# Between the forward and the backward recurrence: row turns in other PSUM banks, loads ahead of crossbar transposes, the last 64 rows moved back, buffers laid out anew

## The chip, the cores and the metric

One NeuronCore of one Trainium2 chip runs the whole program. The metric is the device time in microseconds (us) of one execution. Before the change three executions took 4788.9, 4787.57 and 4790.88 us, with a median of 4788.9 us.

## The reference, cut to what matters

The program computes a block with a memory-augmented attention and a gated feed-forward part, and the gradients of all its inputs. The attention is a recurrence over 64 segments of 32 tokens: each segment sees 8 memory rows and its own 32 rows, and the first 8 rows of its output are the memory of the next segment.

```python
for s in range(n_seg):                                   # 64 segments
    h = concatenate([mem, x[:, s*32:(s+1)*32]], axis=1)   # 8 + 32 rows, D = 640
    q, k, v = h @ Wq, h @ Wk, h @ Wv                      # 32 heads of 128
    p = softmax(where(mask, q @ k.T * scale, -1e9))
    o = (p @ v) @ Wo                                      # 4096 -> 640
    mem, out = o[:, :8], o[:, 8:]
out = x + s * silu(swiglu(xn))                            # s: the attention's output
_, vjp = jax.vjp(f, x, mem0, Wq, Wk, Wv, Wo, w1, w3, w2); grads = vjp(grad_out)
```

## The kernel before, in words

The program is a sequence of phases that share little at their borders. The two that matter here are the forward recurrence, function `recurrence`, and the backward recurrence, function `phase4_Abwd`. Each consists of a serial chain over the 64 segments (`chain`), in whose gaps independent work is placed by hand: `in_order` ties every instruction to its written place on its engine, so each engine runs its list in order and a waiting instruction holds up all that is written behind it on that engine. The DMA queues too are such lists: SP's (`nc.sync`), ScalarE's (`nc.scalar`) and GpSimd's, POOL in the profile (`nc.gpsimd`).

The work in the gaps is attention for the token rows. Three segments make a tile `tl` of 120 rows (96 token rows and 24 memory rows), and a tile has 8 units `(tl, qd)` of 4 heads. A unit goes through: load of q rows (`ld("q", ...)`, tile xq, two buffers), transposes on TensorE (`turn_q`, qpt, L757), scores (xsp), softmax (`soft`, `norm`), transposes of the probabilities (`turn_p`, xpp), product with v (`pv`, xpo), and a store of the output rows into the DRAM array OR. All these PSUM tiles share one ring of five banks, tag "x". The other three banks, bA, bB and bC, belong to the chain.

The stretch between the loops is what the change is about. When the forward chain ends, 13 units (`tail`) still have no scores. They are run in a loop of 15 iterations, and `fill()` calls between their steps draw pieces of other work out of a generator `work1`:

- `out_proj`: the output projection of token rows in blocks of 128 rows. An item is one block and one group of 4 heads, and a block has 8 items. Its OR rows are loaded by POOL into one of four slices `orow` of tile vt, three items ahead (L508). `turn` transposes them (L518) into bC, VectorE copies them into a half of oTm (L519), and 8 matmuls against Wo accumulate the item into bA and bB (L525). After 8 items s_tok is copied out and stored into SR.
- `wq_turn`: 32 head blocks of Wq are transposed on TensorE (L719), also into bC, and copied to WqT.
- `gx_block`: blocks of upstream gradient rows (g0x in this phase, gx in the next; loaded as a crossbar transpose from GS) times WoT into bA and bB (L1045), copied to g0st or gstg and stored in GX0 (called GX in the profile).
- `w_ld`: one piece of a weight that is loaded transposed by the crossbar (`turned_load`, DMA_TRANSPOSE, L270, always on SP's queue). WoT has 16 pieces and WkT has 16.

Rows 1344 to 1855 go through `out_proj` inside the loop, two gradient blocks (rows 1920 to 2047 and 1824 to 1919) follow in the last iterations, and `op(X1, S)`, rows 1856 to 2047, is the last work of the phase.

`phase4_Abwd` begins with small tables (`bdm`, built in gox), zeroed buffers (L1091, and krb at L1398) and a prologue of 19 units of backward attention: per unit `ld` (tiles gqv, gor and gPr, in a ring of six, of which two lie in krb), `turn` (L1290, L1297), `dprob`, `dsoft`, `gmem`, with the other four gradient blocks in between (`gx_work`), and 8 loads of WvT on SP. Before the chain starts, the first ride of token rows (gride) is loaded and copied to gox by POOL (L1113).

SBUF space is handed out by pools. A tile of the new phase that lies over a tile of the old one waits until the old one's users are done.

Of the kernel before, what the change touches and what calls it, by code (L numbers as in the profile page):

```python
# [9 lines left out]
BF16 = mybir.dt.bfloat16  # L10
# [6 lines left out]
P = 128  # L17
# [474 lines left out]
        in_order(k, start)  # L492


def out_proj(k, Wo, x0, x1, acc, pb, orow, oTs, stok, q):

    nc = k.nc
    items = [(x, min(P, x1 - x), qd) for x in range(x0, x1, P) for qd in range(8)]

    def ld(i):  # L500
        if i >= len(items):
            return
        x, w, qd = items[i]
        a = 0
        while a < w:
            tl, r = divmod(x + a, 96)
            n = min(96 - r, w - a)
            q.dma_start(orow[i % len(orow)][a:a + n, :], k.OR[120 * tl + r:120 * tl + r + n, 512 * qd:512 * qd + 512])  # L508
            a += n

    def turn(i):
        if i >= len(items):
            return
        x, w, qd = items[i]
        r = orow[i % len(orow)]
        pt = bview(pb, P, 4, w, bf=True)
        for j in range(4):
            nc.tensor.transpose(pt[:, j, :], r[0:w, j * P:(j + 1) * P], k.ident[0:w, 0:w])  # L518
        nc.vector.tensor_copy(oTs[i % 2][:, :, 0:w], pt)  # L519
# [24 lines left out]


def recurrence(k, W0, W4, Wv, Wk_, Wq, Wo, kTs, vt, hxs, qTs, xPs, PTs, oTm):
    nc, tc = k.nc, k.tc
    D, DC, S, H, HD, T = k.D, k.DC, k.S, k.H, k.HD, k.T
    with tc.tile_pool(name="achain", bufs=1) as ch, \
# [421 lines left out]
        op = lambda x0, x1: out_proj(k, Wo, x0, x1, (bA, bB), bC, orow, oTs, stok, nc.gpsimd)  # L971
        X0, X1 = k.GB0, k.GB0 + 4 * P
        assert X1 <= 96 * (k.NTL - 3) + 96 + 96

        def work1():
            w_alloc("q")
            o = op(X0, X1)
            next(o)
            yield
            for h in range(H):  # L980
                next(o)
                wq_turn(h)
                yield
                next(o)
                yield
            next(o, None)
            w_alloc("k")
            for i, (x0, w) in enumerate(k.GXB[0:2]):
                xs = ch.tile([P, DC, P], BF16, name="g0x", tag=("oride", "fup")[i])
                gx_ld(k, xs, x0, w)  # L990
                for cg in range(4):
                    sg = ch.tile([P, 1024], BF16, name="g0st", tag="stg", bufs=2)
                    for b in range(2):
                        gx_block(k, xs, sg, (bA, bB)[b], WT["o"], x0, w, cg, b, nc.gpsimd)
# [7 lines left out]
        ld("q", *tail[0])  # L1002
        ld("q", *tail[1])
# [13 lines left out]
        ld("q", *tail[3])  # L1017
        ld("v", *tail[0], nc.gpsimd)
        for i in range(len(tail) + 2):
            w_ld(1 if i < 4 else 0)  # L1020
            for f, o, n in ((turn_q, 2, 1), (lambda *u: ld("q", *u), 4, 0), (scores, 1, 1), (soft, 0, 0),
                            (lambda *u: norm(*u, nc.vector), 0, 0), (turn_p, -1, 1), (lambda *u: pv(*u, nc.scalar), -2, 2),
                            (lambda *u: ld("v", *u, nc.gpsimd), 1, 0)):
                if 0 <= i + o < len(tail):
                    f(*tail[i + o])
                fill(n)
        for _ in work:
# [23 lines left out]
def phase4_Abwd(k, out2, W4, WT):  # L1051
# [20 lines left out]
    with tc.tile_pool(name="gst", bufs=1) as st, tc.tile_pool(name="gchain", bufs=1) as ch, \  # L1072
# [2 lines left out]
            tc.tile_pool(name="gpm", bufs=1, space=bass.MemoryType.PSUM) as psm:  # L1075
        NG = 4

        bdm = st.tile([P, 16, 8], BF16, name="bdm")
        goxs = [st.tile([P, DC, 32], BF16, name=f"gox{i}") for i in range(2)]
        bdf = goxs[0][:, 0:4, :].rearrange("p a b -> p (a b)").rearrange("p (a b) -> p a b", b=8)  # L1080
        b16 = st.tile([P, 16], F32, name="b16")
        nc.gpsimd.memset(bdf, 0.0)
        nc.gpsimd.affine_select(out=bdf, in_=bdf, compare_op=ALU.not_equal, fill=1.0, base=0,
                                pattern=[[-1, 16], [-16, 8]], channel_multiplier=1)
        nc.vector.tensor_reduce(b16[:], bdf, axis=AX.X, op=ALU.add)
        nc.vector.tensor_copy(bdm[:], bc_last(b16[:], 8))
        gOTs = [st.tile([P, 4, P], BF16, name=f"gOT{i}") for i in range(2)]
        gors = [st.tile([120, 512], BF16, name=f"gor{i}") for i in range(NG)]
        gdSs = [st.tile([120, 4, P], BF16, name=f"gdS{i}") for i in range(2)]
        for tt in goxs + gOTs + gors + gdSs:  # L1090
            nc.vector.memset(tt[:], 0.0)  # L1091
        krb = st.tile([120, 2, 2048], BF16, name="krb")
        bA, bB, bC = [psm.tile([P, 512], F32, name=f"gbank{i}") for i in range(3)]
        pm = bA
        nc.sync.dma_start(k.m_rows(k.GWO, T - 1).rearrange("r (c d) -> (r c) d", d=160),
                          goxs[(T - 1) % 2][0:32].rearrange("p a b -> p (a b)"))
        rides = {}
        WARM = dict(G4=1)

# [15 lines left out]
        def loads(t):  # L1115
            tl, s = t // 3, t % 3
            ns, nm, nx, n = k.geo(tl)
            vT = ch.tile([P, H, 40], BF16, name="vTt", tag="vTt", bufs=1)
# [19 lines left out]
            krs[t] = kr  # L1138

        def load_xp(t):  # L1140
            xp = ch.tile([P, 8, 2, 32], F32, name="xp", tag="xp", bufs=1)
# [116 lines left out]
        def ld(tl, qd, eng=None):  # L1258
# [6 lines left out]
            g = i % 6 if early else (i - len(pro) + 1) % NG  # L1265
            if g < NG:
                gor = gors[g][:]
                qv = fl.tile([120, 2, 512], BF16, name="gqv", tag="gqv", bufs=4)[:]
                Pr = fl.tile([120, 4, P], BF16, name="gPr", tag="gPr", bufs=4)[:]
# [125 lines left out]
            return gap  # L1395
        todo = pro + todo

        nc.vector.memset(krb[:], 0.0)  # L1398
        xb = krb
        gx = ch.tile([P, 2, DC, P], BF16, name="gx0", tag="vTt", bufs=1)  # L1400

        def gx_work():
            blocks = k.GXB[2:]
# [3 lines left out]
            n = 0  # L1407
            for i, (x0, w) in enumerate(blocks):
                for cg in range(4):
                    sg = ch.tile([P, 1024], BF16, name="gstg", tag=("gstg", "xp")[cg % 2], bufs=1)  # L1410
# [815 lines left out]
```

## Time and profile before

| | us |
|---|---|
| median of three runs (lowest, highest) | 4788.9 (4787.57, 4790.88) |
| the profiled execution | 4788.32 |
| its span in the profile | 4786.6 |
| TensorE (PE) busy in the span | 4491.6 (94%) |
| last PE work before the stretch's first idle time ends at | 1603.36 |
| last matmul of the forward phase ends at | 1790.7 |
| first matmul of the backward chain starts at | 1886.5 |

Times inside the program are us from the span's start. PE is the matmul stream and PEld its weight loads, DVE is VectorE, ACT is ScalarE, SPq and ACTq are the queues in which these engines issue DMAs. "Idle before" or "waited for" says how long an engine stood still and what ended the wait. A line number is that of the kernel before. The granted clock (PEclk) is the share of full speed that TensorE was given.

### The profile page before, as it was taken

The numbers are of one execution on the slowest core, as the hardware profiler recorded it, in microseconds if no ns is written. First come the engines' busy times: TensorE is split into PE (matmuls) and PEld (weight loads), VectorE is DVE, ScalarE is ACT, GpSimd is POOL, SyncE is SP. The second block draws the span as 40 slices with busy tenths as digits, with TensorE's granted clock in tenths as the row PEclk, the third lists the DMA queues.
The fourth block names the chain that finished last, engine by engine and source line by source line (L and its number), as shares of the span: only waits on it lengthen the run. The fifth ranks groups of instructions, "written<-read, shape, count | busy, mean of one in ns | idle before, by whom it ended". The sixth has DMA issues, their size and how long they took to land. (4 is left out here: it accounts for less than half of the span.)

```text
span 4786.6 us, 160294 instructions
## 1 busy us (share of the span) xinstructions
PE 4491.6 (94%) x64504; PEld 2828.7 (59%) x64504; DVE 2246.8 (47%) x7157; ACT 1588.3 (33%) x4360; POOL 2148.4 (45%) x3622
## 2 busy tenths in 40 slices
PE   8998999999999677999999998899999999999999
PEld 4544555555555444666666665666667666666675
DVE  8734666666666424555555553332234322311460
ACT  5432555555544323333333332332233322300000
POOL 6532555555555443445444443653345533411340
PEclk9998999999999898999999999999999999999999
DMA  8773665665555647777777774844355443669673
GB/s 266 231 241 109 180 179 175 178 183 177 176 169 168 149 109 216 202 215 212 213 209 207 210 208 117 213 133 119 107 149 159 132 118 108 184 205 213 153 182 98
DMA packets 972138, 834.82 MB, mean 174 GB/s; under 512 B 518547, under 2 KB 853399, under 8 KB 969433
## 3 DMA queue, kind: packets, MB, share of 16 engines
q1 hardware_dynamic: 757551, 543.98, 40.7%
q0 software_dynamic: 133392, 234.80, 16.6%
q10 hardware_dynamic: 80451, 45.78, 3.7%
q8 instruction: 509, 8.34, 0.8%
q14 instruction: 235, 1.92, 0.1%
HBM read 472.66 MB, written 310.33 MB: 164 GB/s over the span
## 5 line engine op out<-in xcount | busy, mean ns | idle before, releaser
L1600 PE MATMUL wg<-gr,hr 128*128 128x512 bf16 x2400 | 521.7, 379 | 0.0
L1581 PE MATMUL g<-w,ghacc 128*128 128x320 bf16 x3072 | 458.4, 300 | 0.8
L1600 PEld LDWEIGHTS <-hr 128*128 128x128 bf16 x2400 | 234.1, 98 | 278.7
L1581 PEld LDWEIGHTS <-ghacc 128*128 128x128 bf16 x3072 | 288.0, 98 | 103.8 <-ACT ghacc L92 2.2
L306 PEld LDWEIGHTS <-hx 128*32 128x32 bf16 x7680 | 177.1, 96 | 172.8 <-issue 10.1
L90 DVE CAST wgo<-wg 128x512 bf16<-128x512 f32 x72 | 49.8, 692 | 471.2 <-PE wg L1600 471.2
L872 POOL DMA_DIRECT2D OR<-xv x163 | 89.9, 551 | 369.7 <-ACT xv L92 344.6
L90 DVE CAST stg<-bank 128x512 bf16<-128x512 f32 x256 | 177.0, 692 | 165.3 <-PE bank L306 154.0
L1546 POOL DMA_DIRECT2D GSP<-grs x48 | 25.7, 550 | 471.4 <-ACT grs L1538 470.5
L92 ACT COPY ghacc<-t6g 128x768 bf16<-128x768 bf16 (+1 forms) x176 | 137.1, 779 | 296.9 <-PE t6g L1563 294.4
L1294 POOL DMA_DIRECT2D VTD<-gvT x176 | 129.7, 743 | 227.9 <-ACT gvT L1293 204.1
L325 PEld LDWEIGHTS <-gkv 128*8 128x8 bf16 x8192 | 179.5, 87 | 82.8 <-DVE gkv L1165 2.6
L804 ACT ACTIVATE xP<-xsp,xnm 120x120 bf16<-120x120 f32 (+1 forms) x540 | 186.1, 373 | 31.2 <-DVE xnm L786 28.6
L824 POOL TENSOR_TENSOR xP<-xP,xrz 120x480 bf16<-120x480 bf16 x163 | 161.3, 990 | 75.8 <-DVE xrz L823 46.9
L1587 DVE TENSOR_TENSOR ghacc<-ghacc,g 128x320 f32<-128x320 f32 x192 | 93.5, 487 | 209.4 <-PE g L1581 209.4
L92 ACT CAST wgo<-wg 128x512 bf16<-128x512 f32 x48 | 28.1, 585 | 479.8 <-PE wg L1600 421.4
L1323 DVE SCALAR_TENSOR_TENSOR gdS<-gdp,Dx,gPr 120x120 bf16<-120x120 f32 (+1 forms) x680 | 182.9, 331 | 0.0
L1341 POOL DMA_DIRECT2D GXP<-gks x157 | 91.2, 581 | 195.7 <-ACT gks L1339 187.0
L325 PE MATMUL gbank<-WvT,gkv 128*8 128x320 bf16 x4096 | 173.0, 314 | 0.1
L325 PE MATMUL bank<-Wo,oTm 128*32 128x320 bf16 x4032 | 154.8, 308 | 18.5 <-DVE oTm L676 18.5
L306 PE MATMUL bank<-Wq,hx 128*32 128x512 bf16 x2560 | 163.3, 384 | 5.4 <-DVE stg L90 5.4
L325 PE MATMUL gbank<-WkT,gkv 128*8 128x320 bf16 x4096 | 162.2, 299 | 2.4 <-DVE gkv L1165 1.8
(363 smaller groups left out, 10983.9 us busy)
## 6 DMA issues: line engine op xcount, KB each, us to landing
QVS<-stg SPq DMA_DIRECT2D x128, 256.0 KB
gqv<-QVS SPq DMA_DIRECT2D x108, 192.0 KB
vTt<-VTD SPq DMA_DIRECT2D x64, 320.0 KB
PR<-xP POOLq DMA_DIRECT2D x168, 120.0 KB, 3.1
VTD<-gvT POOLq DMA_DIRECT2D x168, 120.0 KB, 3.8
DSR<-gdS POOLq DMA_DIRECT2D x168, 120.0 KB, 3.2
dS<-DSR SPq DMA_DIRECT2D x168, 120.0 KB
P<-PR SPq DMA_DIRECT2D x168, 120.0 KB
```

The source lines that it names most:

```text
L90: return nc.vector.tensor_copy(out, in_)
L92: return nc.scalar.copy(out, in_)
L306: k.nc.tensor.matmul(bank[32 * g:32 * g + 32, :], x[:, dc, :], W[:, dc, c0:c0 + 512], start=(dc == 0), stop=(dc == k.DC - 1), tile_positio ...
L325: k.nc.tensor.matmul(pm[p0:p0 + nq, 0:320], x[:, h, :], W[:, h, 320 * b:320 * b + 320], start=(first and i == 0), stop=(last and i == 15), ...
L804: nc.scalar.activation(Pb[0:n, j, 0:n], sp[0:n, j, :], ACT.Exp, bias=nmx[0:n, j:j + 1], scale=k.scale, accum_out=Z[0:n, j:j + 1])
L824: eng.tensor_tensor(Pb[0:n, :, 0:n], Pb[0:n, :, 0:n], bc_last(rz[0:n], n), ALU.mult)
L1294: nc.gpsimd.dma_start(k.VTD[tl][:, :, h0:h0 + 4, :], vTq[:])
L1323: nc.vector.scalar_tensor_tensor(dS[0:n, j, 0:n], dp[0:n, j, :], Dx[0:n, j:j + 1], Pr[0:n, j, 0:n], op0=ALU.subtract, op1=ALU.mult)
L1341: (nc.sync if (tl, qd) in pro else nc.gpsimd).dma_start(k.GXP[tl, :, qd, 0:ns], ks[:].rearrange("p s i h m -> p s i (h m)"))
L1581: nc.tensor.matmul(pg[:], ring[:, i, j, r0:r0 + P], Ws[qd][i][:, j, 320 * h:320 * h + 320], start=(i == 0 and j == 0), stop=(i == 2 and j ...
L1587: nc.vector.tensor_tensor(a, a, pg[:], ALU.add)
L1600: nc.tensor.matmul(pw[:], hr[:, tl, dc * P:(dc + 1) * P], grs[i][:, tl, :], start=(tl == 0), stop=(tl == NF - 1))
```

## The change: what it does

1. `out_proj` transposes its rows into a tile of the five-bank ring (`obank`) and no longer into bC. bC is left to `wq_turn`.
2. In the last segment's gaps, 4 pieces of WoT are issued where there were 12 by the end of the chain. The q rows of the first two tail units are issued there (gap G1), ahead of the pieces. The other 12 pieces go one per iteration behind the loads of that iteration, and 16 of WkT follow when `wq_turn` is through (Wq's place becomes WkT's).
3. `out_proj` runs 5 blocks, rows 1344 to 1983, inside the loop. Both gradient blocks run behind the loop, and the last 64 rows (1984 to 2047) behind them, with their first three loads issued ahead of the gradient blocks. The first gradient block is loaded (`g_ld(0)`) ahead of WkT's pieces, the second behind them.
4. In `phase4_Abwd` the buffers are static and laid out in another order; krb (120 x 4096 bf16) is zeroed by POOL at the head of its queue and not by VectorE; bdm, the zeroing of gox and its DMA are put off to iteration 8 (`chain_consts`); the loads of four units stand ahead of the gradient rows (gx) on SP.

```diff
-def out_proj(k, Wo, x0, x1, acc, pb, orow, oTs, stok, q):
+def out_proj(k, Wo, x0, x1, acc, bank, orow, oTs, stok, q, done):
...
-        pt = bview(pb, P, 4, w, bf=True)
+        pt = bank(w)
...
                 if t == T - 1:
                     if g == "G1":
                         w_alloc("o")
-                    if g in ("G1", "G2", "G4", "G5"):
-                        w_ld(3)
+                        ld("q", *tail[0])
+                        ld("q", *tail[1])
+                    if g in ("G2", "G4"):
+                        w_ld(2)
...
+        obank = lambda w: ps.tile([P, 4, w], BF16, name="opt", tag="x", bufs=5)
-        X0, X1 = k.GB0, k.GB0 + 4 * P
+        X0, X1 = k.GB0, k.GB0 + 5 * P
...
-            for h in range(H):
-                next(o)
-                wq_turn(h)
-                yield
-                next(o)
-                yield
-            next(o, None)
-            w_alloc("k")
+            for _ in o:
+                if n % 2 == 0 and n < 2 * H:
+                    wq_turn(n // 2)
+                n += 1
+                yield
+                if n == 2 * H:
+                    g_ld(0)
+                    while wfetch:
+                        w_ld(1)
+                    w_alloc("k")
+                elif n > 2 * H:
+                    w_ld(1)
+            g_ld(1)
+            o = op(X1, S)
+            next(o)
             for i, (x0, w) in enumerate(k.GXB[0:2]):
-                xs = ch.tile([P, DC, P], BF16, name="g0x", tag=("oride", "fup")[i])
-                gx_ld(k, xs, x0, w)
...
+            for _ in o:
+                yield
...
         for i in range(len(tail) + 2):
-            w_ld(1 if i < 4 else 0)
...
+            if not WT.get("k"):
+                w_ld(1)
...
-        for _ in op(X1, S):
-            w_ld(1)
-        while wfetch:
-            w_ld(1)
...
+        gors = [st.tile([120, 512], BF16, name=f"gor{i}") for i in range(NG)]
+        gqvs = [st.tile([120, 2, 512], BF16, name=f"gqv{i}") for i in range(NG)]
+        gOTs = [st.tile([P, 4, P], BF16, name=f"gOT{i}") for i in range(2)]
+        vTb = st.tile([P, H, 40], BF16, name="vTt")
...
+        krb = st.tile([120, 2, 2048], BF16, name="krb")
...
-        for tt in goxs + gOTs + gors + gdSs:
+        for tt in gOTs + gors + gdSs:
             nc.vector.memset(tt[:], 0.0)
...
-        nc.vector.memset(krb[:], 0.0)
+        nc.gpsimd.memset(krb[:], 0.0)
...
         work = gx_work()
+        for _ in range(4):
+            ld_next()
         next(work)
-        for _ in range(6):
+        for _ in range(2):
             ld_next()
...
             if i == 8:
+                chain_consts()
                 ride_ld(T - 1)
                 ride(T - 1)
```

More of the change, by code (lines that the diff above doesn't have):

```diff
@@ L507, in ld @@
             n = min(96 - r, w - a)
+            assert tl < k.NTL - 2 or (tl, qd) in done
             q.dma_start(orow[i % len(orow)][a:a + n, :], k.OR[120 * tl + r:120 * tl + r + n, 512 * qd:512 * qd + 512])
@@ L970, in recurrence @@
         stok = lambda: ch.tile([P, D], BF16, name="s_tok", tag="oride")
-        op = lambda x0, x1: out_proj(k, Wo, x0, x1, (bA, bB), bC, orow, oTs, stok, nc.gpsimd)
-        X0, X1 = k.GB0, k.GB0 + 4 * P
-        assert X1 <= 96 * (k.NTL - 3) + 96 + 96
+        obank = lambda w: ps.tile([P, 4, w], BF16, name="opt", tag="x", bufs=5)
+        done = {(k.NTL - 2, qd) for qd in SPL[0]}
+        op = lambda x0, x1: out_proj(k, Wo, x0, x1, (bA, bB), obank, orow, oTs, stok, nc.gpsimd, done)
+        X0, X1 = k.GB0, k.GB0 + 5 * P
         def work1():
@@ L979, in work1, with g_ld @@
             yield
-            for h in range(H):
-                next(o)
-                wq_turn(h)
-                yield
-                next(o)
-                yield
-            next(o, None)
-            w_alloc("k")
+            g0 = []
+            def g_ld(i):
+                xs = ch.tile([P, DC, P], BF16, name="g0x", tag=("fup", "oride")[i])
+                gx_ld(k, xs, *k.GXB[i])
+                g0.append(xs)
+            n = 0
+            for _ in o:
+                if n % 2 == 0 and n < 2 * H:
+                    wq_turn(n // 2)
+                n += 1
+                yield
+                if n == 2 * H:
[8 more added lines that the diff above has]
+            next(o)
             for i, (x0, w) in enumerate(k.GXB[0:2]):
-                xs = ch.tile([P, DC, P], BF16, name="g0x", tag=("oride", "fup")[i])
-                gx_ld(k, xs, x0, w)
                 for cg in range(4):
@@ L993, in work1 @@
                     for b in range(2):
-                        gx_block(k, xs, sg, (bA, bB)[b], WT["o"], x0, w, cg, b, nc.gpsimd)
+                        gx_block(k, g0[i], sg, (bA, bB)[b], WT["o"], x0, w, cg, b, nc.gpsimd)
                         w_ld(1)
                         yield
+            for _ in o:
+                yield
         def fill(n=1):
@@ L1001, in recurrence @@
         work = work1()
-        ld("q", *tail[0])
-        ld("q", *tail[1])
         fill()
@@ L1025, in recurrence @@
                     f(*tail[i + o])
+                    if o == -2:
+                        done.add(tail[i + o])
                 fill(n)
+            if not WT.get("k"):
+                w_ld(1)
+        assert next(work, 0) is None
         for _ in work:
             pass
-        for _ in op(X1, S):
-            w_ld(1)
-        while wfetch:
-            w_ld(1)
+        assert not wfetch
         in_order(k, start)
@@ L1076, in phase4_Abwd @@
         NG = 4
+        gors = [st.tile([120, 512], BF16, name=f"gor{i}") for i in range(NG)]
+        gqvs = [st.tile([120, 2, 512], BF16, name=f"gqv{i}") for i in range(NG)]
+        gOTs = [st.tile([P, 4, P], BF16, name=f"gOT{i}") for i in range(2)]
+        vTb = st.tile([P, H, 40], BF16, name="vTt")
+        goxs = [st.tile([P, DC, 32], BF16, name=f"gox{i}") for i in range(2)]
         bdm = st.tile([P, 16, 8], BF16, name="bdm")
-        goxs = [st.tile([P, DC, 32], BF16, name=f"gox{i}") for i in range(2)]
+        xpb = st.tile([P, 8, 2, 32], F32, name="xp")
+        gPrs = [st.tile([120, 4, P], BF16, name=f"gPr{i}") for i in range(NG)]
+        gdSs = [st.tile([120, 4, P], BF16, name=f"gdS{i}") for i in range(2)]
+        krb = st.tile([120, 2, 2048], BF16, name="krb")
         bdf = goxs[0][:, 0:4, :].rearrange("p a b -> p (a b)").rearrange("p (a b) -> p a b", b=8)
         b16 = st.tile([P, 16], F32, name="b16")
[L1082 to L1089, printed above, removed]
-        for tt in goxs + gOTs + gors + gdSs:
+        for tt in gOTs + gors + gdSs:
             nc.vector.memset(tt[:], 0.0)
-        krb = st.tile([120, 2, 2048], BF16, name="krb")
         bA, bB, bC = [psm.tile([P, 512], F32, name=f"gbank{i}") for i in range(3)]
         pm = bA
-        nc.sync.dma_start(k.m_rows(k.GWO, T - 1).rearrange("r (c d) -> (r c) d", d=160),
-                          goxs[(T - 1) % 2][0:32].rearrange("p a b -> p (a b)"))
         rides = {}
@@ L1117, in loads @@
             ns, nm, nx, n = k.geo(tl)
-            vT = ch.tile([P, H, 40], BF16, name="vTt", tag="vTt", bufs=1)
+            vT = vTb
             nc.sync.dma_start(vT[:], k.VTD[tl][:, s])
@@ L1140, in load_xp @@
         def load_xp(t):
-            xp = ch.tile([P, 8, 2, 32], F32, name="xp", tag="xp", bufs=1)
+            xp = xpb
             nc.sync.dma_start(xp[:], k.GXP[t // 3, :, :, t % 3])
@@ L1267, in ld @@
                 gor = gors[g][:]
-                qv = fl.tile([120, 2, 512], BF16, name="gqv", tag="gqv", bufs=4)[:]
-                Pr = fl.tile([120, 4, P], BF16, name="gPr", tag="gPr", bufs=4)[:]
+                qv, Pr = gqvs[g][:], gPrs[g][:]
             else:
@@ L1396, in phase4_Abwd, with chain_consts @@
         todo = pro + todo
-        nc.vector.memset(krb[:], 0.0)
+        def chain_consts():
+            nc.gpsimd.memset(bdf, 0.0)
+            nc.gpsimd.affine_select(out=bdf, in_=bdf, compare_op=ALU.not_equal, fill=1.0, base=0,
+                                    pattern=[[-1, 16], [-16, 8]], channel_multiplier=1)
+            nc.vector.tensor_reduce(b16[:], bdf, axis=AX.X, op=ALU.add)
+            nc.vector.tensor_copy(bdm[:], bc_last(b16[:], 8))
+            for tt in goxs:
+                nc.gpsimd.memset(tt[:], 0.0)
+            t = T - 1
+            nc.sync.dma_start(k.m_rows(k.GWO, t).rearrange("r (c d) -> (r c) d", d=160),
+                              goxs[t % 2][0:32].rearrange("p a b -> p (a b)"))
+        nc.gpsimd.memset(krb[:], 0.0)
         xb = krb
-        gx = ch.tile([P, 2, DC, P], BF16, name="gx0", tag="vTt", bufs=1)
+        gx = vTb[:].rearrange("p h c -> p (h c)").rearrange("p (i a b) -> p i a b", i=2, a=DC)
+        xs2 = xpb[:].rearrange("p a b c -> p (a b c)").bitcast(BF16)
         def gx_work():
@@ L1409, in gx_work @@
                 for cg in range(4):
-                    sg = ch.tile([P, 1024], BF16, name="gstg", tag=("gstg", "xp")[cg % 2], bufs=1)
+                    sg = ch.tile([P, 1024], BF16, name="gstg", tag="gstg", bufs=1)[:] if cg % 2 == 0 else xs2
                     for b in range(2):
```

## The prediction, made before the changed kernel ran

> **What bounds the kernel now.** I read the 40 slices of the page first, then busy time by stage, then waits and queues inside the stretch that the diff touches.
>
> ```profile
> PE   8998999999999677999999998899999999999999
> ```
>
> TensorE is busy nearly everywhere, so a gain must come from its few idle places. Slices 14 to 16 (6, 7, 7) are the stretch between the loops. Cut at the ends of its stages (us; PE, PEld, DVE, ACT and POOL busy, PE clock, DMA share, GB/s):
>
> ```profile
> 1603.40:1623.70 20.30, 0.00 (x0) 0.02 (x1) 0.72 (x2) 0.58 (x1) 7.28 (x13) 0.50 1.12 217
> 1624.00:1723.70 99.70, 77.34 (x808) 53.90 (x806) 34.82 (x104) 43.01 (x149) 49.91 (x97) 0.95 0.38 94
> 1723.70:1790.70 67.00, 46.48 (x292) 26.71 (x292) 13.25 (x34) 8.24 (x21) 23.09 (x45) 0.90 0.62 142
> 1790.70:1886.50 95.80, 65.05 (x620) 38.56 (x619) 45.60 (x258) 31.94 (x110) 35.17 (x60) 0.80 0.76 226
> ```
>
> PE stands idle for 20.3, 22.4, 20.5 and 30.8 us: first at the start, then in the tail loop, then in the crossbar and last-row stage, then in the backward prologue. No other engine is near full, so these are waits. The list of waits for 1595 to 1890 (waiter, what it waited for: total us, times, longest):
>
> ```profile
> PE qpt L757 <- DMA xq<-QVS: 20.3, 1, 20.3
> PE bank L518 <- DMA vt<-OR: 12.9, 5, 6.9
> PE bank L719 <- DVE oTm L519: 11.8, 10, 2.0
> PE bank L1045 <- DMA g0x<-GS: 10.0, 2, 7.1
> PE gvpt L1290 <- DMA gqv<-QVS: 8.2, 1, 8.2
> POOL gox L1113 <- DMA gride<-GS: 11.9, 1, 11.9
> ```
>
> SP's and POOL's queues at the start (start us, duration, engine, line):
>
> ```profile
> 1601.29 5.87 SPq L270 DMA_TRANSPOSE WoT<-in_A_Wo_dram  x3
> 1607.25 0.53 SPq L604 DMA_DIRECT2D QVS<-stg  x1
> 1607.83 12.75 SPq L270 DMA_TRANSPOSE WoT<-in_A_Wo_dram  x6
> 1620.63 0.72 SPq L245 DMA_DIRECT2D xq<-QVS  x1
> ...
> 1611.49 0.56 POOL L571 DMA_DIRECT2D QVM<-QVS  x1 [4.71 <-DMA QVS<-stg]
> 1612.04 3.06 POOL L508 DMA_DIRECT2D vt<-OR  x6
> ```
>
> A crossbar piece holds SP for about 2 us, and the first q load stands behind nine. POOL's OR loads wait separately, behind QVM, which waits for a store that SP held back too.
>
> **The change part by part.**
>
> *Start.* SP's order becomes: two q units (4 DMAs, about 2.2 us), v loads (2.3), two pieces (3.8), the QVS store, two pieces. From 1593.1 the q loads are out by 1595.3 and the store goes at about 1602, instead of 1607.25. It landed 4.2 us after issue (1607.25 to 1611.49), so by about 1606.2. POOL's queue is then at QVM anyway (its QM issue is at 1606.20), and the OR loads start near 1607.3 instead of 1612.04. The first item's two take 1.0 us to issue and 2.5 (median landing in the loop) to 5.3 (here, beside the pieces) to land: 1611 to 1613.6. Transposes of q no longer wait, but the first row turn does, until about 1612 instead of 1624.06: **-12 us** (-9 to -15). The idle time shrinks to about 8 us; it is not gone.
>
> *Tail loop.* In bC each turn waited for the other kind's copy; the 11.8 us in ten waits go. Their cover is good: in the new order a row turn's copy is needed only an item later. In exchange the ring of five takes 6.5 tiles per iteration and not 4. One tile, the score bank, is held from `scores` to the last exp. The program's waits show a row turn behind `pv` waiting for just that exp in some iterations. The exps of a unit are 4 x (0.38 + 0.2) us and its max is 0.65, about 3 us after its place, when PE has done about 3 us of other work. The trace has no such wait, so I bound it: 0, or 1 us in each of 15 iterations; I take 3 us, since ACT is busy for 43 of 99.7 us. The waits for OR in the loop (1.9 and 2.5 us) and the 3.3 us for s_tok remain. One crossbar piece per iteration of about 7.6 us, behind that iteration's loads, is covered by two iterations of lead on q. Net **-9 us** (-14 to 0). The eight items moved into the loop cost what they cost before, 8 x (1.25 + 0.06 us seen between items): no gain or loss.
>
> *Crossbar and last rows.* Idle waits here are 7.1 + 2.9 us for g0x, 6.9 + 1.0 for OR, 1.5 for a g0st buffer. They come from PE running out of other work while SP needs 13.65 + 15.80 us for WkT's 16 pieces. After the change the pieces start when the last Wq block is turned (at 1720.9 before), and 9 items (9 x 1.6), the rest of attention (4), and the first gradient block (10) lie beside them: 28.4 us against 29.5. The second gradient block's load stands behind all pieces and needs 2.9 us (1727.92 issue to 1730.80 use): about 4 us of wait. The last 64 rows' loads are covered by the gradient blocks; in their queue the fourth stands behind the last GX store, about 1.5 us. Here a rule and a row part. The Trainium skill (DMA: Bandwidth & Descriptors, Anatomy of one DMA — SWDGE path, two cost components) puts one DMA at 2.0 us plus bytes over 436 GB/s, an estimate of 2.2 us for a load of 96 KB: three items ahead (4.9 us) hides each OR load beside the pieces at no cost. The trace's list of DMA issues has medians of 2.5 us in the loop (1640 to 1720) but 5.3 us beside WoT's pieces (1595 to 1625); with 1 us of issue that exceeds 4.9 by 1.4 us, for up to 9 items: 12 us. By the rule 0, by the row at most 12; I take 4, because the wait also lets SP's pieces get ahead and so comes off the 4 us of g0x. GX stores meet the pieces as before: 3 us. So 4 + 1.5 + 4 + 3 = 12.5 less 1 of overlap = 11.5 us instead of 20.5: **-9 us** (-18 to +3). Waits of 7 us went with slow clock (0.72 in the 10 us after the first, 0.66 around the second); of the low-clock time in the middle two stages (about 5% of 77 and 10% of 46 us, 8.5 us), I take half back: **-4 us** (-7 to 0).
>
> *Border.* Before, the last matmul ends at 1790.7 and the first turn starts at 1798.96. New: both copies of s_tok (0.48 us), SR's issue, its landing 2.0 us later (2.6 in all). The new program has SP, VectorE and POOL all wait for that. On POOL krb's memset comes next, ahead of the four QVM loads. Here is the second rule: the skill (VectorE: DVE Perf Modes, Zero memsets can be issued as uint32) says a memset takes a cycle per element and that VectorE may clear two bf16 as one word. It speaks against this edit, and the trace has both forms:
>
> ```profile
> L1398 DVE MEMSET krb<- 120x2048 uint32 x1 | 1.8, 1765 | 0.4 <-issue 0.4
> L475 POOL MEMSET kT<- 128x3840 bf16 x1 | 3.3, 3317 | 0.0
> ```
>
> By the POOL row 4096 elements take 3.54 us. If POOL cleared words too it would be 1.8, and the border would stay at 8.2. By the row: 2.6 + 3.54 + 3.3 (landing of gqv<-QVM) = 9.4: +1.2 us. The gradient rows now stand behind twelve loads, which took 6.55 us (1796.40 to 1802.95): 2.7 + 6.55 + 2.9 = 12.2 us after the end, where the first gradient matmul began after 8.96. PE is full from there to 1827, so this shifts the prologue: **+3.2 us**, the 1.2 inside it (0 to +5).
>
> *Prologue.* The 8 WvT loads and their DMA share of 0.9 stay. `chain_consts` adds to POOL and VectorE some 1.5 us (the tables took 0.20, 0.40, 0.23 and 0.24; two memsets 0.24 each) in front of gox, but POOL stood 11.9 us there, waiting for gride. That cover holds. On SP one small DMA (0.3 us), with its wait for the memset, is put ahead of gride, so that chain ends later: **+1 us** (0 to +3). The removed table work stood beside SR's landing and gives nothing.
>
> Sum: -12 - 9 - 9 - 4 + 3.2 + 1 = -29.8 us. The profiled execution took 4788.32 us, 1.7 around its span, so 4758.5; the median is 0.6 above it, so 4759.
>
> **The rivals.**
>
> *The loop's gain is eaten beside the pieces.* WkT's 29.5 us are fixed. If PE arrives early it waits for the second g0x, and OR loads at 5.3 us stall it: the third stage gives nothing, nor do 3 us of clock. -30 + 9 + 3 = -18: 4771 us. For it: DMA share 1.0 to 1.1 in 1730 to 1760. Against: 14 us of moved projection now lie there.
>
> *Only the start's q loads help.* If the QVS store, between the pieces, lands as late as before, OR loads start at 1612, the row turn at 1618: -6; with the loop's 9 lost to the ring, border and prologue at +8: -6 - 9 - 1 + 8 = -8, 4781 us, no change. This is also the case that the change does not do what it says: waits only move to the next release.
>
> *Slower: the ring of five.* Every one of 48 row turns takes a ring bank. If each waits for the exp that frees a score bank, in-order PE, VectorE and ScalarE run in step. Gain without it is 33 us (3 were charged already), so it decides from 33/48 = 0.7 us per turn. At 1.1 us: 53 - 33 = +20, 4809 us. For it: 6.5 tiles in five banks. Against: in the loop before, no wait of PE for a ring tile or for bC was over 2.0 us, and ScalarE is 43% busy.
>
> **How the numbers follow.** Forecast (-45 to -21) 0.57; eaten beside the pieces (-21 to -10) 0.24; no change (within 9.6 us, 0.2%, about what a measurement of this kernel can tell from none) 0.09; the ring, slower, 0.10. Faster 0.81, same 0.09, slower 0.10. The range takes the first two cases to their ends: 4744 to 4779.
>
> **What would show it.** Right: the wait of xq (20.3) gone and PE's first idle time about 8 us, released by vt<-OR; no oTm wait at L719's successor; last forward matmul some 34 us earlier; the border wait on gqv near 9.4 us and the first gx matmul about 12 us after the end; krb's memset 3.5 us on POOL. Wrong: idle time of row turns in the ring (opt) above 10 us in sum, a g0x wait above 10 us, or a prologue over 105 us.

## The result, and the profile after

| | before | after |
|---|---|---|
| median of 9 runs, us | 4792.89 (4779.51 to 4804.0) | 4769.33 (4759.59 to 4779.03) |
| profiled execution, us | 4788.32 | 4766.39 |
| span of that execution, us | 4786.6 | 4764.5 |

The runs of before here are those of the front table and six more. The ratio is 0.9951 (95% interval 0.9936 to 0.9966): faster, by about 24 us. The forecast was 4759, its range 4744 to 4779.

The changed kernel by stage (each cut is at the same piece of work as before: PE's last work before the idle time, its first work after it, the end of the last Wq block's turn, the last forward matmul, the first matmul of the backward chain; given are length; PE, PEld, DVE, ACT and POOL busy; PE clock, DMA share, GB/s). The stages are the idle start, the tail loop, the crossbar and last rows, and the border with the prologue:

```profile
1606.80:1614.08 7.28, 0.01 (x1) 0.03 (x1) 0.36 (x2) 0.69 (x2) 6.28 (x12) 0.50 0.94 231
1614.08:1711.65 97.57, 74.83 (x807) 54.21 (x808) 34.55 (x103) 42.35 (x147) 53.91 (x105) 0.94 0.58 129
1711.65:1770.30 58.65, 46.80 (x292) 26.49 (x290) 13.27 (x33) 8.43 (x21) 19.96 (x39) 0.88 0.74 153
1770.30:1868.50 98.20, 64.20 (x609) 38.42 (x616) 44.11 (x255) 31.42 (x110) 39.12 (x63) 0.80 0.74 221
```

With before cut at the same events (1603.37, 1623.71, 1723.12, 1790.71, 1886.49), the stages went from 20.34 to 7.28 us, from 99.41 to 97.57, from 67.59 to 58.65, and from 95.78 to 98.20. These four differences, -13.1, -1.8, -8.9 and +2.4, make -21.4 of the span's -22.1. The odd one is the second: PE's idle time in the loop is 97.57 - 74.83 = 22.7 us, where it was 99.41 - 77.09 = 22.3. The list of PE's waits, 1595 to 1870 (waiter, what it waited for: total us, times, longest), says what took the place of oTm:

```profile
PE opt L519 <- DMA vt<-OR: 28.7, 17, 7.3
PE gvpt L1303 <- DMA gqv<-QVM: 9.2, 1, 9.2
...
PE gbank L1062 <- DMA vTt<-GS: 4.1, 1, 4.1
PE bank L1062 <- DVE g0st L90: 4.1, 1, 4.1
...
PE bank L1062 <- DMA g0x<-GS: 2.3, 1, 2.3
```

The waits of 20.3 us for xq and of 11.8 us for oTm are gone. The row turns' waits for rows in the loop alone, after and then before:

```profile
PE opt L519 <- DMA vt<-OR: 24.3, 14, 7.3
PE bank L518 <- DMA vt<-OR: 5.0, 3, 2.5
```

Of the 24.3 us, 7.3 are the start's, which leaves 17.0 us where before had 5.0. So the time that PE had spent waiting for oTm was not saved; PE now waits for the next thing that is late. GpSimd's timeline in the loop shows how the rows come (start, duration, line, in brackets the idle time ahead and what ended it):

```profile
1653.38 1.03 POOL L509 DMA_DIRECT2D vt<-OR  x2
1658.34 0.55 POOL L826 DMA_DIRECT2D PR<-xP  x1 [3.92 <-ACT xv L92]
1658.88 1.01 POOL L509 DMA_DIRECT2D vt<-OR  x2
...
1703.46 0.54 POOL L826 DMA_DIRECT2D PR<-xP  x1 [5.69 <-ACT xP L805]
1703.99 1.01 POOL L509 DMA_DIRECT2D vt<-OR  x2
```

No row load is issued for over 4 us at the first place, and for over 6 us at the second, because the store of P ahead of it in GpSimd's order waits. PE turns an item's rows about every 3 us (33 such turns in the 97.6 us). A lead of three items, some 9 us, is then in large part used up before the load is issued. The longest wait for rows inside the loop follows the second place. It ends with the pair of loads issued at 1703.99, for the next pair leaves only at 1706.00:

```profile
1706.86 0.39 PE L519 MATMUL opt<-ident,vt 128*128 128x128 bf16 x4 [4.09 <-DMA vt<-OR]
```

PE was ready for these rows at 1702.77, before their loads were issued.

### The profile page after: what moved, and what is told of

Read it like the earlier page. It is cut to its first block, busy times and chain, and to the rows that moved or that the text cites. A ratio compares the mean times of both kernels' runs of the same rounds, so it can differ in the third digit from the quotient of the medians.

```text
span 4764.5 us, 159990 instructions
## 1 busy us (share of the span) xinstructions
PE 4452.5 (93%) x64223; PEld 2829.8 (59%) x64504; DVE 2245.4 (47%) x7154; ACT 1587.8 (33%) x4360; POOL 2152.3 (45%) x3625
## 3 DMA queue, kind: packets, MB, share of 16 engines
q0 software_dynamic: 133392, 234.80, 16.6%
## 5 line engine op out<-in xcount | busy, mean ns | idle before, releaser
L325 PEld LDWEIGHTS <-gkv 128*8 128x8 bf16 x8192 | 179.9, 87 | 83.6 <-DVE gkv L1179 2.7
L1616 DVE TENSOR_TENSOR ghacc<-ghacc,g 128x320 f32<-128x320 f32 x192 | 93.5, 487 | 209.0 <-PE g L1610 209.0
```

The lines of the kernel that those rows point to most:

```text
L325: k.nc.tensor.matmul(pm[p0:p0 + nq, 0:320], x[:, h, :], W[:, h, 320 * b:320 * b + 320], start=(first and i == 0), stop=(last and i == 15), ...
L1616: nc.vector.tensor_tensor(a, a, pg[:], ALU.add)
```

## The experiments

The stages of all kernels, from their profiled executions (us; the start's idle time, the loop, the crossbar and last rows, border and prologue), with PE's idle time in the loop where a reading rests on it, and the ratio to before.

| kernel | start | loop (PE idle) | last rows | border, prologue | median, ratio (interval) |
|---|---|---|---|---|---|
| before | 20.3 | 99.4 (22.3) | 67.6 | 95.8 | 4788.2 to 4794.39 in four sets of runs |
| after | 7.3 | 97.6 (22.7) | 58.7 | 98.2 | 4769.33, 0.9951 (0.9936-0.9966) |
| a1_pieces_late | 7.3 | 98.7 (21.5) | 57.4 | 100.9 | 4767.24, 0.9940 (0.992-0.996) |
| a2_p_store_sp | 7.1 | 94.1 (16.6) | 59.4 | 100.4 | 4757.29, 0.9917 (0.9896-0.9937) |
| a3_ahead_five | 7.1 | 81.8 (8.8) | 59.5 | 93.2 | 4747.10, 0.9896 (0.9875-0.9917) |
| c1_ahead_four | 7.5 | 83.6 (10.6) | 56.8 | 99.9 | 4738.67, 0.9898 (0.9879-0.9916) |
| a4_ring_alone | 19.2 | 98.7 (21.0) | 68.8 | 93.7 | 4789.61, 0.9991 (0.9981-1.0000) |
| b2_ahead_five_alone | 20.2 | 98.0 (19.8) | 68.9 | 95.4 | 4790.87, 1.0000 (0.9990-1.0011) |
| c4_ring_and_ahead | 21.0 | 79.8 (7.0) | 69.6 | 92.4 | 4769.40, 0.9956 (0.9939-0.9972) |
| b1_q_first | 14.2 | 102.1 | 67.5 | 95.6 | 4791.65, 0.9999 (0.9988-1.0011) |
| c3_start_alone | 7.2 | 102.6 | 71.2 | 94.1 | 4777.46, 0.9975 (0.9961-0.9989) |
| b3_border | 6.7 | 101.3 (22.8) | 55.8 | 94.4 | 4754.27, 0.9930 (0.991-0.995) |
| b4_ahead_and_border | 7.9 | 80.1 (8.5) | 57.3 | 93.5 | 4742.38, 0.9899 (0.9881-0.9917) |
| c2_first_rows_early | 5.7 | 82.5 | 57.4 | 96.0 | 4743.76, 0.9903 (0.9888-0.9918) |

A stage with the same code differs by up to 4 us between kernels (the loop of after and of b3_border: 97.6 and 101.3, with clocks of 0.94 and 0.89), and border and prologue by 8; differences below that are not read from one row. PE's idle time in the loop scatters less (22.7 and 22.8 in these two). Each ratio is to the runs of before made with it, so kernels are compared by ratio and not by median.

**Where did the loop's 9 us go?** There were three suspects: GpSimd's order (T1 in the expectations), the crossbar pieces (T2) and the short lead (T3).

*a1_pieces_late.*

```diff
-            if not WT.get("k"):
-                w_ld(1)
```

> The changed kernel without the one WoT crossbar piece per iteration of the tail loop: those 12 pieces are all issued at the end of the loop, ahead of WkT's 16. Where did the loop's expected 9 us go? T2 (the pieces beside the OR loads lengthen their landing, now 2.8 to 4.3 us a load): waits of PE's row turns for vt<-OR inside the loop fall from 17 us to about 5 as before the change, and the loop shrinks from 97.7 to about 88 us; the last stage then has 28 pieces to wait for and grows from 58.5 by 10 to 20 us, so the total is up by 0 to 10 us. T1 (the OR loads stand on POOL's in-order queue behind stores of P that wait for the softmax): the waits in the loop stay near 17 us and the loop near 97 us, and the total is up by 10 to 20 us. T3 (prefetch of three items is too short whatever else runs): as T1 in the loop.

SyncE was free to run ahead, so the twelve pieces ran within the loop's last 33 us, not after it, and the last stage did not grow. SyncE's timeline:

```profile
1681.27 25.05 SPq L270 DMA_TRANSPOSE WoT<-in_A_Wo_dram  x12
```

That leaves a stretch of 66 us of loop without any piece. PE's waits in it (1615.3 to 1681.2):

```profile
PE opt L519 <- DMA vt<-OR: 15.3, 8, 7.3
```

and the same stretch of the changed kernel (1614.2 to 1680), with a piece per iteration:

```profile
PE opt L519 <- DMA vt<-OR: 16.9, 9, 7.3
```

Less the start's 7.3, that is 8.0 against 9.6 us. The pieces do lengthen the landing (medians from issue to landing in 1617 to 1700: 3.5, 4.3 and 2.9 us for 96, 64 and 32 KB in after; 2.7, 2.3 and 2.7 here), but taking them away saves 1.6 us of waits. T2 falls as the main cause.

*a2_p_store_sp.*

```diff
-  (lambda *u: norm(*u, nc.vector), 0, 0)
+  (lambda *u: norm(*u, nc.vector, nc.sync), 0, 0)
```

> The changed kernel with the tail loop's stores of P issued from SyncE's queue instead of GpSimd's, so that no OR load stands behind a store that waits for the softmax. T1 (the queue order holds the OR loads back): waits of row turns for vt<-OR in the loop fall from 17 us to under 7, loop about 88 us, total down by about 9 us. T2 (transfers are slowed by the pieces): waits stay at 14 to 20 us, total within 3 us; the stores now hold SyncE's queue while the softmax runs, so later q loads or pieces may come late by a few us.

PE's waits in its loop:

```profile
PE opt L519 <- DMA vt<-OR: 14.9, 8, 7.1
PE opt L519 <- issue: 4.6, 2, 2.5
```

14.9 - 7.1 + 4.6 = 12.4 us instead of 17.0, and PE's idle time in the loop falls from 22.7 to 16.6: a miss between the two expectations. The experiment did not free GpSimd's queue, though. In this loop the queue stood still for about 43 us in all, in after's loop for about 42. By the profile the place of the stores of P was taken above all by the load of the next v rows, which waits for a store of OR rows to empty its buffer (GpSimd's waits, 1613.6 to 1707.6):

```profile
POOL xv L747 <- DMA OR<-xv: 17.8, 4, 5.4
```

So the stores of P are a part of the delay, and what GpSimd's order costs as a whole is not settled by this run. The stage behind it had one wait of 8.2 us for rows, where after's longest was 2.7, but took no longer than the scatter (59.4 us). The four stages sum to 261.0 us against 261.7 in after, so the lower total (4757) does not come from them; its interval just touches that of after.

*a3_ahead_five* and *c1_ahead_four* load further ahead. They take two more slices from a buffer that is idle there (c1: one more), and as many loads ahead as slices less one.

```diff
-    for i in range(3):
+    ahead = len(orow) - 1
+    for i in range(ahead):
         ld(i)
...
-        ld(i + 3)
+        ld(i + ahead)
...
+        orow += [fl.tile([P, 512], BF16, name=f"orx{i}", tag="kr", bufs=2)[:] for i in range(2)]
```

> The changed kernel with the OR loads five items ahead in six slices instead of three ahead in four (two slices from a buffer that is idle there). Whether the loads are late because they are issued late or because they land slowly, two items more of lead (about 3 us or more) should cover them: waits of row turns for vt<-OR fall from 17 us in the loop to under 6, the wait at the start of 7.3 us stays, the last stage gives back 0 to 4 us; total down by about 10 us, to 4758. If instead the transfers are limited by throughput (share of DMA engines 0.58 in the loop), a longer lead does not help and waits stay above 12 us.

> The changed kernel with four OR loads ahead in five slices: the dose between three (waits of row turns for vt<-OR of 17 us in the loop) and five (under 4). An item takes about 1.6 us of PE's time, and GpSimd's stores of P stand up to 4.4 us in front of the loads behind them. If the lead counts item by item, the waits are about half, 8 us, and the loop about 89 us (97.6 with three, 81.8 with five), total near 4758. If the loads come in bursts behind a held store, of which four fit once and five always, it is nearer one of the ends: under 4 us or above 13.

PE's waits in a3_ahead_five's loop (the first 7.1 us are the start's):

```profile
PE opt L519 <- DMA vt<-OR: 7.7, 2, 7.1
...
PE opt L519 <- DMA orx<-OR: 0.5, 1, 0.5
```

7.7 - 7.1 + 0.5 = 1.1 us of waits for rows are left of 17.0; the loop is 15.8 us shorter, and PE's idle time in it 8.8 us instead of 22.7. The DMA share rose from 0.58 to 0.69 in it, so throughput was not the limit. With four ahead the loop's waits are 11.0 - 7.5 = 3.5 us and the loop is 83.6 us: one item more is nearly enough, as the second of c1's two expectations had it. The totals of the two kernels overlap, and both ratios lie clear of after's; a3's gain is about twice the 10 us expected. So the rows were late because their loads left too late for the time they take to land. How much of that is GpSimd's holding and how much the landing, a longer lead does not tell, since it covers both.

**Why did it not show before?** Before had one turn bank and three items ahead. Each part alone, on the kernel before, and both:

*a4_ring_alone.*

```diff
-        pt = bview(pb, P, 4, w, bf=True)
+        pt = bank(w)
...
+        obank = lambda w: ps.tile([P, 4, w], BF16, name="opt", tag="x", bufs=5)
```

> The kernel before with one part of the change alone: the row turns take their PSUM bank from the ring of five that the units use, not from one fixed bank. Tells what the ring is worth without the pieces in each iteration. All theories: the oTm waits (11.8 us in ten) go. T2 (pieces): before's loop holds only four pieces, so OR waits stay near 5 us, the loop shrinks from 99.1 to about 90 us and the total by 8 us. T1 and T3 (queue order or a short lead): PE reaches its row turns earlier, the OR waits rise to 12 us or more and the loop shrinks by under 3 us, total within 3 us. The rival of my prediction (ring too small): waits for the ring's tiles over 10 us.

*b2_ahead_five_alone* has the diff of a3_ahead_five on the kernel before; *c4_ring_and_ahead* has both diffs.

> The kernel before with five OR loads ahead in six slices, nothing else: row turns stay in the fixed bank. Tells whether ring and lead add up or need each other. The ring alone gave 0.7 us of the loop (98.7 against 99.4), ring and lead and the rest of the change 17.7 (81.8). A: they need each other (a row turn waits for whichever comes last, the buffer of the turn before or its rows): oTm waits stay at 10 us or more, the loop shrinks by 2 to 5 us. B: the lead is all that counts: the loop shrinks by 12 us or more and the oTm waits shrink too. In both the last stage loses 3 to 7 us, since its waits for vt<-OR (6.9 and 1.0) go.

> The kernel before with the ring of five banks and five OR loads ahead together, nothing else. Alone, neither moved the loop (98.7 and 98.0 us against 99.4). If each only uncovers the other's wait, the two together take both away: loop about 84 us, waits for vt<-OR under 4 us and none for oTm; total down by 10 to 15 us, less what the stage behind it takes back, since WkT's pieces there (29.5 us) do not start earlier than their buffer is free and PE then waits for g0x: last stage 68 up to 75 us. If the loop stays above 95 us, its shrinking in a3_ahead_five came from the moved pieces or rows, not from these two.

PE's waits in the three loops. The ring alone:

```profile
PE opt L518 <- DMA vt<-OR: 14.1, 10, 4.1
...
PE opt L518 <- ACT xP L804: 1.7, 1, 1.7
```

the lead alone:

```profile
PE bank L720 <- DVE oTm L519: 14.2, 12, 2.0
```

both:

```profile
PE bank L525 <- DVE s_tok L90: 4.3, 3, 3.4
PE bank L525 <- DVE oTm L519: 2.5, 4, 0.9
```

This is the finding of the study. The waits of the row turns and Wq turns were, before, 11.8 us for oTm and 5.0 for rows, 16.8 in all. With the ring alone they are 14.1, all for rows. With the lead alone they are 14.2, all for oTm. With both there is none of either (the oTm row left there is another wait, of the matmuls at L525). The loops are 99.4, 98.7, 98.0 and 79.8 us: -0.7, -1.4, and together -19.6. Two chains of nearly the same length ran side by side, one that frees the buffer and one that brings the rows; cutting either shows the other. Of the 19.6 us, 15.3 are PE's idle time (22.3 to 7.0). The other 4.3 are its busy time, which fell from 77.1 to 72.8 us for the same 807 matmuls at nearly the same clock (0.95 and 0.94); why is not shown. The total follows: 0.9991, 1.0000 and 0.9956. The expectation that the lead alone would also shorten the last stage by 3 to 7 us was missed (68.9 us against 67.6). The ring's own price, the part of my slower rival, is small: in the first of these lists one wait of 1.7 us for a score bank's exps, beside one of 0.3 us for another bank. And c4's loop is as short as a3's without the moved pieces and rows, so these gave the loop nothing that shows.

**The start.** *b1_q_first* loads two q units ahead of the twelve pieces; *c3_start_alone* also leaves only four pieces there and puts the other twelve into the loop. The diff is c3's; of it b1 has the moved ld lines only.

```diff
                         w_alloc("o")
-                    if g in ("G1", "G2", "G4", "G5"):
-                        w_ld(3)
+                        ld("q", *tail[0])
+                        ld("q", *tail[1])
+                    if g in ("G2", "G4"):
+                        w_ld(2)
...
-        ld("q", *tail[0])
-        ld("q", *tail[1])
...
-            w_ld(1 if i < 4 else 0)
+            w_ld(1 if i < 12 else 0)
```

> The kernel before with one part of the change alone: the first two q units are loaded ahead of the twelve WoT crossbar pieces, which keep their places. Splits the start's 13 us between the q loads and the pieces taken away. A: if the store of QVS behind three pieces and the six pieces after it decide (the rival 'only the start's q loads help'), the wait for xq (20.3 us) goes, but the first row turn then waits for vt<-OR until 4 to 7 us before its old place: start 13 to 16 us instead of 20.3, total down by 4 to 7. B: if the q loads are the whole of it, the start shrinks to about 7 us as in the changed kernel, total down by 13.

> The kernel before with the change's whole start and nothing else: q loads first, four WoT pieces there instead of twelve, the other twelve one per iteration of the loop. With b1_q_first (start 14.2 us, first row turn released by vt<-OR) it splits the start's 13 us: the q loads gave 6, the pieces moved should give the other 7, start about 7.3 us. The loop keeps the fixed bank and three items ahead: about 99 us if the pieces there cost nothing (a1_pieces_late says so), 102 or more if they do. Total down by 10 to 13 us if no later stage takes it back.

b1_q_first's first row turn, in PE's timeline:

```profile
1626.45 0.59 PE L518 MATMUL bank<-ident,vt 128*128 128x128 bf16 x4 [14.17 <-DMA vt<-OR]
```

So the q loads alone give 6 us (case A), and the pieces moved behind the QVS store give the other 7 (7.21 us in c3_start_alone). b1's 6 us are not seen in its total (4 to 7 were expected), c3's 13 us are (-11 us). Both have loops of 102 to 103 us, about 3 longer than before, of which 2 are busy time of PE (79 us against 77, at clocks of 0.92 and 0.93 against 0.95); what set the clock there was not found.

*c2_first_rows_early* is b4_ahead_and_border (below) with the first two items' loads issued in the chain's last iteration.

```diff
+                    if g == "G5":
...
+                        first.append(out_proj(..., done, 2))
+                        next(first[1])
```

> The kernel b4_ahead_and_border with the first two items' OR loads (into the two slices that the chain does not use) issued in the chain's last iteration, ahead of the last stores of P and of QM and QVM, instead of behind them. Attacks the 7 to 8 us that PE still waits at the start in every version. If GpSimd's queue order is what holds the first row turn: the start falls from 7.9 to 1 to 4 us (the third item's rows still come at the old time), total down by 4 to 6 us, to 4737. If the rows themselves arrive late beside the pieces: start stays above 6 us, total unchanged.

GpSimd's timeline shows the early loads, then the place where they stood before:

```profile
1605.85 2.06 POOL L509 DMA_DIRECT2D orx<-OR  x4
...
1610.34 0.57 POOL L577 DMA_DIRECT2D QVM<-QVS  x1
1610.95 0.55 POOL L509 DMA_DIRECT2D vt<-OR  x1
```

and PE's timeline the turn that waits for them:

```profile
1612.19 0.58 PE L519 MATMUL opt<-ident,orx 128*128 128x128 bf16 x4 [5.73 <-DMA orx<-OR]
```

Five us earlier in the queue gave 2 us of start (7.9 to 5.7): beside the pieces these loads took 6.1 to 6.3 us to land (medians of 32 and 96 KB, 1604 to 1613). In b4, where they leave after the pieces, they took 2.5 and 3.1 us (medians of 32 and 96 KB, tile vt, 1604 to 1620). Leaving earlier thus traded time in the queue for time of landing. The total did not move. The start's rest in c2 is the landing, near what the second expectation had.

**The border.** *b3_border* undoes two edits in the changed kernel; *b4_ahead_and_border* adds a3_ahead_five's lead.

```diff
-        nc.gpsimd.memset(krb[:], 0.0)
+        nc.vector.memset(krb[:], 0.0)
...
-        for _ in range(4):
-            ld_next()
         next(work)
-        for _ in range(2):
+        for _ in range(6):
             ld_next()
```

> The changed kernel with two edits at the border undone: krb is cleared on VectorE and not on GpSimd (3.51 us), and the two gradient-row transposes are issued ahead of the four units' twelve loads and not behind them. Both were costed in the prediction (1.2 and 3.2 us in all). Expected: first turn 8.3 us after the last forward matmul instead of 9.24, first gradient matmul at about 9 us instead of 13.76 and no wait of 4 us for vTt<-GS; the prologue ends 3 to 4.5 us earlier (border and prologue 94 to 95 us instead of 98.2), total down by 3 to 5 us. Rival: the prologue's end is set by gride (9.7 to 13 us of wait on GpSimd), not by the gradient blocks: then the first matmul comes earlier and the stage is within 1 us of 98.

> The changed kernel with five OR loads ahead in six slices and the border of b3_border together. If the two are independent: loop about 82 us as in a3_ahead_five, border and prologue 3 to 4 us shorter than there (93.2), total about 4744 us. Rival: as the pieces' stage is limited by SyncE (59 us in every version so far), nothing beyond a3_ahead_five's 4747.

The changed kernel's SyncE queue, the last of the twelve loads and the gradient rows behind them:

```profile
1779.73 0.37 SPq L1294 DMA_DIRECT2D gPr<-PR  x1
1780.14 2.56 SPq L270 DMA_TRANSPOSE vTt<-GS  x2
```

b3_border's first turn, in PE's timeline:

```profile
1774.30 0.29 PE L1303 MATMUL gvpt<-ident,gqv 40*128 40x40 bf16 x4 [8.79 <-DMA gqv<-QVS]
```

With the rows in front, the first gradient matmul starts 9.6 us after the last forward matmul instead of 13.8, and border and prologue take 94.4, 93.5 and 96.0 us in the three kernels that have this, where the five with the changed order take 93.2 to 100.9 (mean 98.5) and the six with the old code 92.4 to 95.8 (mean 94.5). The means differ by 4 us, but the ranges overlap. The memset costs nothing that shows: the first turn comes 8.8, 8.8 and 9.8 us after the end without it on GpSimd (b3, b4, c2) and 8.8 to 9.2 with it, since in these three it is gqv<-QVS that comes last. b3's total is down by more than the 3 to 5 us expected (4754.27), but its interval overlaps that of after. b4's total of 4742.38 is below after's 4769.33, but not to be told from a3's or c1's.

## Why the prediction was right, and which term was not

*Start, -12: right.* It fell by 13.1 us, and PE's first idle time is 7.3 us, released by vt<-OR, where about 8 was said. The two halves of the step, q loads and fewer pieces ahead of the QVS store, are shown by b1_q_first and c3_start_alone. SyncE's store went at 1604.55 and not at 1602, and the row loads at 1610.36 and not near 1607.3: the chain itself ended 3.4 us later in this execution.

*Tail loop, -9: the term that was mis-sized; it gave 1.8.* That is within the scatter of a stage, and PE's idle time in the loop did not fall at all (22.3 to 22.7 us). What failed is the sentence "The waits for OR in the loop (1.9 and 2.5 us) and the 3.3 us for s_tok remain": it kept the rows' waits at their old size. The oTm waits went as said (0.3 us is left). But the rows' 5 us were not a fixed amount: they were what was left of the rows' lateness after PE had spent 11.8 us waiting for oTm. The runs show 14.1 us in their place on the kernel before (a4) and 17.0 in after. The last forward matmul came 20.4 us earlier (1790.71 to 1770.30), or 23.8 counted from the chain's end, not 34. The 3 us charged for the ring were a smaller thing: 1.3 us in after's loop. A sign of being wrong that I had named did appear: the row turns in the ring stood idle for more than 10 us in sum (25.6 us in the loop, the start's 7.3 included), though for rows and not for a ring tile.

*Crossbar and last rows, -9: right.* The stage took 58.65 us where 67 - 9 = 58 was said, and the waits (from the list for this stage and PE's timeline) are near the terms of the sum: 2.3 us for g0x (4 said), 3.3 for rows beside WkT's pieces (4 said), 1.1 for the fourth load of the last rows (1.5 said), 4.1 for a g0st buffer (3 said). Before, g0x alone had cost 10.0 us. Over all kernels with the new order the stage takes 55.8 to 59.5 us, with the old 67.5 to 71.2. c3 and c4 have parts of the change in the start and the loop and stay at 71.2 and 69.6, so as far as these runs show it is the new order of this stage that pays; which of its moves, no run separates. The estimate of 2.2 us for a load of 96 KB from the Trainium skill (DMA: Bandwidth & Descriptors, Anatomy of one DMA — SWDGE (gpsimd) path, two cost components) was too low for this stage: even row loads of 64 KB took 4.7 us to land, those of 32 KB 2.7 (medians, 1711.65 to 1770), and three items ahead did not hide each load. Five ahead did not either (3.8 us of waits for rows in a3's stage), so the lead is not the whole reason here, and the rest stays open.

*Clock, -4: not seen.* The two stages have 0.94 and 0.88 after 0.95 and 0.90. The loop of other kernels had 0.89 (a2, b3) to 0.96 (b4) with the same work, so the clock was nothing from which half of the low-clock time could be taken back.

*Border, +3.2, and prologue, +1: together 4.2, measured 2.4 in this pair and about 4 over all kernels.* The parts shifted: the first gradient matmul came 13.8 us after the end (12.2 said), and the first turn came after 9.24 us (9.4 said), but only 0.4 us of that went when krb's memset, 3.51 us on GpSimd as the row said, was taken from there (b3, 8.79), since gqv<-QVS comes next. gride's wait of 11.9 us on GpSimd stayed, as did the cover it gives.

*The rivals.* The ring as a bound is refuted (a4, and -19.6 us in c4 with the same ring). "Only the start's q loads help" describes b1_q_first, not the change. "The loop's gain is eaten beside the pieces" named a time, 4771, near the measured 4769.33, but not the place: the third stage gave all that it was to give, and the loop's gain was lost within the loop. The forecast's band (-45 to -21) holds the result at its lower end. That is in part luck: of the 29.8 us summed, the loop's 9 and the clock's 4 did not come, and the number stayed in the range because the range was wide and the start, the last rows and the border came out near or better than said.

## What to carry to other kernels

When one wait in a loop is removed, ask what was late but hidden under it, and size that before taking the gain: the waits in a list are those that came last, and a second chain as long as the first shows only as the small remainder. Try the two fixes together: here each alone was worth about 1 us and both about 20. Count the lead of a prefetch on the queue that issues it, with what is held in front of it there, and not in items of the consumer; here one slice more was nearly enough. Look, too, whether another instruction takes the place of the one that you move out of a queue.

## What the runs showed of the hardware

- The granted clock of a stage did not follow PE's idle time. In the loop it was 0.95 with 22.3 us idle (before), 0.94 with 8.8 (a3), 0.96 with 8.5 (b4) and 0.89 with 16.6 (a2).
- Row loads of 96 KB and 32 KB took 6.3 and 6.1 us to land beside three WoT transposes (c2, 1604 to 1613), and 3.1 and 2.5 us behind them (b4, 1604 to 1620). In the loops with four pieces the medians were 2.5 to 3.1 and 2.1 to 2.8 us (before, a4, b1, b2, c4), in those with twelve 2.6 to 4.3 and 2.2 to 4.3 us (after, a2, a3, b3, b4, c1, c2, c3). Size mattered less than what ran beside them.
